# The last store of a fused attention and gated-MLP kernel, in two partition halves from two engines

## The chip, the cores and the metric

The kernel runs on one core of a Trainium2 chip. A core has TensorE (matrix products, into PSUM), VectorE, ScalarE and GpSimd (elementwise work), SyncE, which here issues the transfers, and 16 DMA engines that move data between HBM and the on-chip SBUF. Engines run their own instruction lists and wait for each other by semaphores. The metric is the device time of one execution in microseconds (us); the kernel before takes 222.05 us (median of 3 runs, 221.95 to 222.31).

## The reference

The input x is 2048 tokens by 512 columns. It is normalised once, goes through two branches, and both results are added to x:

```
xn = layernorm(x)                                   # 2048 x 512, bf16
# A: linear attention, 32 heads of 16
q, k, v = split(xn @ wqkv)
phi(t)  = [softmax(t @ w_phi), softmax(-(t @ w_phi))]     # 32 features per head
o       = phi(q) @ (phi(k)^T v) / (phi(q) @ sum(phi(k)) + 1e-6)
A       = o @ wo
# B: gated MLP, 512 -> 1792 -> 512
B       = ((xn @ w_gate) * (xn @ w_up)) @ w_down
out     = x + A + B
```

The output has the shape of x, in bf16: 2 MB.

## The kernel before, in words

Tokens are handled in 16 tiles of 128 (`NT`), in four groups of four. After the loads, a first phase normalises the tiles, makes keys and values, and sums phi(k)^T v over all tiles; units of the gated MLP (`unit`, lines 268 to 280; one of 14 column blocks for one group of 512 tokens) are mixed in so that TensorE always has work. A second loop (lines 444 to 453) goes over the tiles again: `attend(n)` makes the attention result of a tile and has it transposed by a DMA, `qproj` prepares a later tile, and `fin(n - 2)` finishes a tile that is two behind. The order on every engine and on the DMA queue is the order of the program text (line 102 takes the planning out of the framework's hands), so what is written last runs last on each engine.

`fin(n, cuts)` (lines 287 to 300) does the last step for one tile. For each stretch of output columns between two cuts it accumulates 14 products of the MLP with `w_down` (line 293) and 4 of the attention with `wo` (line 296) in one PSUM bank, adds x on VectorE into the bf16 tile `o_sb` (line 299), and stores it (line 300). For 15 tiles there is one stretch of 512 columns. The last tile is called with cuts at 0, 384 and 512 (line 456), so that its last store has 128 columns: 128 partitions (token rows) by 256 bytes, 32 KB.

All transfers in this kernel, loads, transposes and stores, are issued by SyncE (`nc.sync`); ScalarE issues none. SyncE's stores are preceded in its list by the transposes of the attention tiles. After the last store SyncE's list has only the waits at the end of the program (line 482), in which it waits for all transfers before the engines meet in a barrier.

Of the kernel before, what the change touches and what calls it, by code (L numbers as in the profile page):

```python
# [21 lines left out]
def kernel(  # L22
# [12 lines left out]
    nc = tc.nc  # L35
    P = 128
    S, D = A_x.shape[-2], A_x.shape[-1]
# [12 lines left out]
    def token_views(ap):  # L50
        rows = ap.flatten_outer_dims()
        first = rows[0:TT, :].rearrange("(n p) d -> p n d", p=P)
        rest = rows[TT:S, :].rearrange("(p n) d -> p n d", p=P)
        return lambda lo, hi: first[:, lo:hi, :] if hi <= GT else rest[:, lo - GT:hi - GT, :]

    x_view = token_views(A_x)
    out_view = token_views(out)
# [29 lines left out]
    for lo in (0, 2):  # L87
        nc.sync.dma_start(out=wv[:, lo:lo + 2, :],
                          in_=A_wqkv[lo * P:(lo + 2) * P, 2 * D:3 * D].rearrange("(c p) f -> p c f", p=P))
# [58 lines left out]
    def bank(name, dt=F32, n=TT):  # L148
        return ps_s.tile([P, n], dt, name=name, tag="s")
# [137 lines left out]
    def fin(n, cuts=(0, D)):  # L287
        T, t4 = n // GT, n % GT
        for lo, hi in zip(cuts, cuts[1:]):
            w = hi - lo  # L290
            ps = bank("fin")[:, 0:w]
            for f in range(FC):
                nc.tensor.matmul(ps, lhsT=hTs[T][:, f, t4 * P:(t4 + 1) * P], rhs=wd[:, f, lo:lo + w],  # L293
                                 start=(f == 0), stop=False)
            for c in range(DC):
                nc.tensor.matmul(ps, lhsT=oTs[n][:, c, :], rhs=wo[:, c, lo:lo + w],  # L296
                                 start=False, stop=(c == DC - 1))
            o_sb = opool.tile([P, w], BF16, name=f"o_sb{w}")
            nc.vector.tensor_tensor(out=o_sb[:], in0=ps, in1=xall[:, n, lo:lo + w], op=ALU.add)  # L299
            nc.sync.dma_start(out=out_view(n, n + 1)[:, 0, lo:lo + w], in_=o_sb[:])  # L300


    warm = bank("warm")
# [120 lines left out]
    with tc.tile_pool(name="ps_ab", bufs=1, space=PSUM) as ps_ab, \  # L424
# [19 lines left out]
        for n in range(NT):  # L444
            attend(n)
            if n + 5 < NT:
                qproj(n + 5)
            if n < 2:
                ffn(2 - n)
                continue  # L450
            fin(n - 2)
            if n >= 4:
                ffn(2)
        ffn(len(units))
        fin(NT - 2)
        fin(NT - 1, cuts=(0, 3 * P, D))


# [28 lines left out]
```

## Time and profile before

The profile is of one execution, taken by the hardware profiler.

| what | value |
|---|---|
| median of 3 runs | 222.05 us (221.95 to 222.31) |
| the profiled execution's own time | 221.94 us |
| its span, first to last instruction | 220.2 us |
| TensorE busy | 214.5 us, 97% of the span |
| VectorE, ScalarE, GpSimd busy | 63%, 40%, 33% |
| granted clock of TensorE (mean) | 0.998 |
| stores | 15 of 128 KB, one of 96 KB, one of 32 KB |
| last addition on VectorE | 217.50 to 217.79 us |
| last store issued | 217.82 us |

How to read it: a row of the timeline has the start in us from the span's start, the duration, the engine (PE is TensorE, DVE is VectorE, ACT is ScalarE, SPq is SyncE's issuing of DMAs), the source line, the operation with output and inputs, and behind the bracket what ended the engine's idle time. An issue row is the time in which the engine hands the transfer over, not the time in which the data move. "To landing" is from the start of the issue to the last report of the DMA engines that the data are there; each of the 16 engines reports by raising the store's semaphore by one. In a table of stretches the columns are the stretch, its length and TensorE's busy time (with the number of instructions), then weight loads, VectorE, ScalarE and GpSimd, the granted clock, the share of the 16 DMA engines and GB/s.

### The profile page before, as it was taken

Reading aid. Unit: us, or ns where it says so; the run is one execution under the profiler, and the core shown is the slowest. Engines: PE = TensorE matmul, PEld = TensorE weight load, DVE = VectorE, ACT = ScalarE, POOL = GpSimd, SP = SyncE. Lnnn points to the kernel's source line nnn. Section 1 sums busy time; section 2 is a strip of 40 time slices with the busy share of each in tenths; the row PEclk is TensorE's granted clock in tenths of the full one; section 3 lists DMA queues with packets and bytes.
Section 4 is the critical chain, followed back from the end, with each engine's and each line's share of the span. In section 5 each row is a group of like instructions: output and inputs, shape, how many; then the busy total and the mean of one; then the engine's idle time right before and its main releaser. Section 6 shows DMA issues by size and latency. Waiting matters only on the chain.

```text
span 220.2 us, 3489 instructions
## 1 busy us (share of the span) xinstructions
PE 214.5 (97%) x1285; PEld 104.4 (47%) x1309; DVE 138.4 (63%) x237; ACT 88.2 (40%) x162; POOL 72.1 (33%) x62
## 2 busy tenths in 40 slices
PE   7999999999999999999999999999999999999995
PEld 2564444445444444444544444444444444454443
DVE  5657985885579685756589964197655745445321
ACT  2635486559755876545354221231322323100000
POOL 5300555455336653536333633033033033000000
PEclk9999999999999999999999999999999999999999
DMA  5999994404201223010205945214431431522611
GB/s 171 261 306 383 368 225 59 95 1 49 49 0 33 42 54 65 18 34 0 48 1 100 119 95 113 58 24 95 98 72 24 95 71 27 91 53 71 69 30 48
DMA packets 47233, 19.91 MB, mean 90 GB/s; under 512 B 37488, under 2 KB 46960, under 8 KB 47088
## 3 DMA queue, kind: packets, MB, share of 16 engines
q1 hardware_dynamic: 47216, 19.69, 39.6%
q8 instruction: 10, 0.16, 0.3%
q14 instruction: 7, 0.06, 0.1%
HBM read 8.67 MB, written 2.10 MB: 49 GB/s over the span
## 4 chain that ended last, share of the span: by engine, by line
PE 94%; DVE 2%; DMA 1%; issue 1%; POOL 0%; ACT 0%; DVEq 0%
PE fin L293 22%; PE u L275 22%; PE g L275 21%; PE fin L296 6%; PE pv L240 6%; PE q L240 6%; PE k L240 6%; PE ab L430 2%; PE kv L333 2%; DMA xall<-in_A_x_dram 1%; DVE stats L155 1%; PE pq L231 1%; DVE sums L252 1%; PE tp L213 0%; DVE hT L280 0%
## 5 line engine op out<-in xcount | busy, mean ns | idle before, releaser
L275 PE MATMUL u<-xnT,wu 128*128 128x512 bf16 (+1 forms) x229 | 57.7, 372 | 0.4
L275 PE MATMUL g<-xnT,wg 128*128 128x512 bf16 (+1 forms) x222 | 56.7, 371 | 0.4
L280 DVE TENSOR_TENSOR hT<-u,g_sb 128x512 bf16<-128x512 f32 (+1 forms) x58 | 37.4, 649 | 27.3 <-PE u L275 18.0
L279 ACT CAST g_sb<-g 128x512 bf16<-128x512 f32 (+1 forms) x58 | 33.3, 573 | 48.2 <-PE g L275 48.1
L252 DVE TENSOR_REDUCE sums<-e 128x64 f32<-128x1024 f32 x32 | 38.9, 1215 | 20.7 <-ACT e L249 20.7
L293 PE MATMUL fin<-wd,hT 128*128 128x512 bf16 (+2 forms) x234 | 50.9, 366 | 0.3
L256 POOL TENSOR_TENSOR phiq<-e,rs 128x1024 bf16<-128x1024 f32 x16 | 31.0, 1935 | 61.4 <-DVE rs L254 53.1
L256 POOL TENSOR_TENSOR phik<-e,rs 128x1024 bf16<-128x1024 f32 x16 | 30.9, 1934 | 48.2 <-DVE rs L254 46.2
L275 PEld LDWEIGHTS <-wu 128*128 128x128 bf16 x232 | 22.6, 98 | 25.7
L293 PEld LDWEIGHTS <-hT 128*128 128x128 bf16 x238 | 22.4, 98 | 24.8
L275 PEld LDWEIGHTS <-wg 128*128 128x128 bf16 x232 | 21.9, 98 | 23.4
L240 PEld LDWEIGHTS <-xnT 128*128 128x128 bf16 x192 | 17.3, 97 | 18.2 <-ACT xnT L215 1.1
L299 DVE TENSOR_TENSOR o_sb<-fin,xall 128x512 bf16<-128x512 f32 (+2 forms) x17 | 11.2, 656 | 22.3 <-PE fin L296 22.2
L248 ACT ACTIVATE e<-q 128x512 f32<-128x512 f32 x16 | 9.5, 596 | 26.1 <-PE q L240 20.7
L254 DVE RECIPROCAL rs<-sums 128x64 f32<-128x64 f32 x32 | 17.7, 553 | 3.1
L240 PE MATMUL pv<-wv,xnT 128*128 128x512 bf16 x62 | 16.4, 379 | 0.4 <-ACT xnT L215 0.2
L296 PE MATMUL fin<-wo,oT 128*128 128x512 bf16 (+2 forms) x68 | 16.6, 366 | 0.0
L240 PE MATMUL k<-W1k,xnT 128*128 128x512 bf16 x63 | 16.2, 379 | 0.0
L240 PE MATMUL q<-W1q,xnT 128*128 128x512 bf16 x60 | 15.9, 378 | 0.1
L322 ACT CAST vt<-pv 128x512 bf16<-128x512 f32 x14 | 8.3, 591 | 10.9 <-PE pv L240 10.9
L248 ACT ACTIVATE e<-k 128x512 f32<-128x512 f32 x16 | 9.6, 597 | 7.0 <-PE k L240 6.6
L439 DVE TENSOR_TENSOR otok<-ab,rden 128x512 bf16<-128x512 f32 x16 | 11.1, 691 | 0.6
(46 smaller groups left out, 117.4 us busy)
## 6 DMA issues: line engine op xcount, KB each, us to landing
out_dram<-o_sb SPq DMA_DIRECT2D x15, 128.0 KB, 1.9
wd<-in_B_w_down_dram SPq DMA_DIRECT2D x1, 1792.0 KB, 15.4
wg<-in_B_w_gate_dram SPq DMA_DIRECT2D x2, 640.0 KB, 7.0
wu<-in_B_w_up_dram SPq DMA_DIRECT2D x2, 640.0 KB, 8.1
xall<-in_A_x_dram SPq DMA_DIRECT2D x1, 1024.0 KB, 12.0
wv<-in_A_wqkv_dram SPq DMA_DIRECT2D x2, 256.0 KB, 3.9
wg<-in_B_w_gate_dram SPq DMA_DIRECT2D x2, 256.0 KB, 4.9
wu<-in_B_w_up_dram SPq DMA_DIRECT2D x2, 256.0 KB, 5.3
```

Of the source, the lines that this page charges most:

```text
L240: nc.tensor.matmul(ps, lhsT=xnT[:, j, n * P:(n + 1) * P], rhs=w[:, j, :], start=(j == 0), stop=(j == DC - 1))
L248: nc.scalar.activation(out=e[:, :, 0, :], in_=pfv, func=AF.Exp, scale=1.0)
L252: nc.vector.tensor_reduce(out=sums[:], in_=ev, axis=AX.X, op=ALU.add)
L254: nc.vector.reciprocal(out=rs[:].rearrange("p a b -> p (a b)"), in_=sums[:])
L256: nc.gpsimd.tensor_tensor(out=phi[:].rearrange("p g (x f) -> p (g x) f", f=DH), in0=ev, in1=rs[:].to_broadcast((P, 2 * H, DH)), op=ALU.mult)
L275: nc.tensor.matmul(ps, lhsT=w[:, c, f * P:(f + 1) * P], rhs=xnT[:, c, T * TT + lo:T * TT + hi], start=(c == 0), stop=(c == DC - 1))
L279: nc.scalar.copy(out=g_sb[:, 0:hi - lo], in_=pss[0])
L280: nc.vector.tensor_tensor(out=hTs[T][:, f, lo:hi], in0=pss[1], in1=g_sb[:, 0:hi - lo], op=ALU.mult)
L293: nc.tensor.matmul(ps, lhsT=hTs[T][:, f, t4 * P:(t4 + 1) * P], rhs=wd[:, f, lo:lo + w], start=(f == 0), stop=False)
L296: nc.tensor.matmul(ps, lhsT=oTs[n][:, c, :], rhs=wo[:, c, lo:lo + w], start=False, stop=(c == DC - 1))
L299: nc.vector.tensor_tensor(out=o_sb[:], in0=ps, in1=xall[:, n, lo:lo + w], op=ALU.add)
L439: nc.vector.tensor_tensor(out=o_tok[:].rearrange("p (b h d) -> p b h d", b=2, d=DH), in0=abv[:, :, :, 0:DH], in1=rden[:].to_broadcast((P, ...
```

## The change

In `fin`, the store of a stretch stays as it is, except for the last stretch of a tile that is cut more than once. That is one store in the whole program: columns 384 to 511 of tile 15. It is issued as two: partitions 0 to 63 of `o_sb` by SyncE, partitions 64 to 127 by ScalarE. Each has 64 rows of 256 bytes, 16 KB, and goes to its own rows of the output.

```diff
@@ -297,7 +297,11 @@
                                  start=False, stop=(c == DC - 1))
             o_sb = opool.tile([P, w], BF16, name=f"o_sb{w}")
             nc.vector.tensor_tensor(out=o_sb[:], in0=ps, in1=xall[:, n, lo:lo + w], op=ALU.add)
-            nc.sync.dma_start(out=out_view(n, n + 1)[:, 0, lo:lo + w], in_=o_sb[:])
+            if hi < D or len(cuts) == 2:
+                nc.sync.dma_start(out=out_view(n, n + 1)[:, 0, lo:hi], in_=o_sb[:])
+            else:
+                for eng, rows in ((nc.sync, slice(0, P // 2)), (nc.scalar, slice(P // 2, P))):
+                    eng.dma_start(out=out_view(n, n + 1)[rows, 0, lo:hi], in_=o_sb[rows, :])
```

## The prediction

> **What bounds the kernel now.** I read the page's first and fourth parts first (busy shares, and the chain that ended last), then the timeline of the last microseconds, then the queue's issues and what the queue waited for, and last a table of stretches over the two stores that can be told apart. The page says which engine carries the run:
>
> ```profile
> span 220.2 us, 3489 instructions
> PE 214.5 (97%) x1285; PEld 104.4 (47%) x1309; DVE 138.4 (63%) x237; ACT 88.2 (40%) x162; POOL 72.1 (33%) x62
> ...
> PE 94%; DVE 2%; DMA 1%; issue 1%; POOL 0%; ACT 0%; DVEq 0%
> ...
> out_dram<-o_sb SPq DMA_DIRECT2D x1, 96.0 KB, 1.6
> out_dram<-o_sb SPq DMA_DIRECT2D x1, 32.0 KB, 1.4
> ```
>
> TensorE is busy for 97% of the span and makes 94% of the chain; nothing in this change touches it. What is left for a change of the last store is the stretch after the last matmul. The two store rows differ from the other fifteen: 96 KB and 32 KB, because the last tile is cut at column 384; the 32 KB one is the store in question, and it lands 1.4 us after its issue. The timeline of the end:
>
> ```profile
> 216.50 0.56 DVE L299 TENSOR_TENSOR o_sb<-fin,xall 128x384 bf16<-128x384 f32 x1 [2.23 <-PE fin L296]
> ...
> 217.08 0.39 PE L296 MATMUL fin<-wo,oT 128*128 128x128 bf16 x4
> ...
> 217.50 0.29 DVE L299 TENSOR_TENSOR o_sb<-fin,xall 128x128 bf16<-128x128 f32 x1 [0.45 <-PE fin L296]
> ...
> 217.82 0.33 SPq L300 DMA_DIRECT2D out_dram<-o_sb  x1
> ```
>
> The last matmuls end at about 217.47, the last addition runs from 217.50 to 217.79, and SyncE issues the last store from 217.82 to 218.15. After that only this store is under way. What ends it is in the queue's own waits over the last 4 us:
>
> ```profile
> SPq L300 <- DVE o_sb L299: 2.7, 2, 2.4
> SPq L482 <- DMA out_dram<-o_sb: 1.0, 1, 1.0
> SPq L482 <- PEq L482: 0.6, 2, 0.4
> ```
>
> L482 is the end of the program, where SyncE waits for every transfer; 1.0 us of that is the wait for this store. ScalarE is free for the new issue: its last instruction in the whole trace is this one, 29 us before the end:
>
> ```profile
> 188.12 0.59 ACT L279 CAST g_sb<-g 128x512 bf16<-128x512 f32 x1 [1.14 <-PE g L275]
> ```
>
> Stretches of the store of 128 KB issued at 210.41 (first four rows) and of the last store (the others); the last two columns are the share of the 16 DMA engines and GB/s:
>
> ```profile
> 210.41:210.74 0.33, 0.33 (x3) 0.14 (x2) 0.00 (x0) 0.00 (x0) 0.00 (x0) 1.00 0.00 0
> 210.74:211.23 0.49, 0.49 (x4) 0.21 (x3) 0.00 (x0) 0.00 (x0) 0.00 (x0) 1.00 0.00 0
> 211.23:211.76 0.53, 0.53 (x4) 0.28 (x3) 0.00 (x0) 0.00 (x0) 0.00 (x0) 1.00 0.73 247
> 211.76:212.11 0.35, 0.35 (x4) 0.13 (x2) 0.00 (x0) 0.00 (x0) 0.00 (x0) 1.00 0.00 0
> 217.82:218.15 0.33, 0.00 (x0) 0.00 (x0) 0.00 (x0) 0.00 (x0) 0.00 (x0) 1.00 0.63 205
> 218.35:218.64 0.29, 0.00 (x0) 0.00 (x0) 0.00 (x0) 0.00 (x0) 0.00 (x0) 1.00 0.00 0
> 218.64:218.92 0.28, 0.00 (x0) 0.00 (x0) 0.00 (x0) 0.00 (x0) 0.00 (x0) 1.00 0.55 117
> 218.92:219.26 0.34, 0.00 (x0) 0.00 (x0) 0.00 (x0) 0.00 (x0) 0.00 (x0) 1.00 0.00 0
> 219.26:220.19 0.93, 0.00 (x0) 0.00 (x0) 0.00 (x0) 0.00 (x0) 0.00 (x0) 0.60 0.00 0
> ```
>
> So a store is made of four parts. For the last one: issue 0.33 (the traffic seen in that row is the 96 KB store before it, whose packets end at 218.34), then 0.49 in which nothing moves, 0.28 of packets, 0.34 until the last of its 16 engines has reported: 1.44 us, 217.82 to 219.26. The store of 128 KB has the same 0.33 and 0.49, 0.53 of packets, and its last report 1.69 after its start. Only the packet part scales with size. Behind the last report come 0.93 us of closing waits and barriers.
>
> **The change part by part.** One store of 128 rows by 256 bytes becomes two of 64 rows by 256 bytes. The bytes, the matmuls, the addition and all earlier stores stay: the test in the code holds only for the last piece of the last tile.
>
> Size alone. From 32 to 128 KB the time to the last report grows from 1.44 to 1.69, 0.25 us for 96 KB, that is 0.0026 us per KB. A 16 KB half would by that line land in 1.44 - 0.04 = 1.40 us. Carried to no bytes at all, the line leaves 1.35, so the whole possible gain from less data per store is below 0.09 us, and 0.04 is my value, since half of the 32 KB remains in each.
>
> Both halves meet on the same engines. In the packet records the store's 128 rows are 8 packets of 256 bytes on each of 16 engines, 18 ns each at a pitch of about 14 ns. If the halves run together over all 16, each engine has the same eight to move, and even the 0.04 is not there; I keep it as the lower end.
>
> A rule of the Trainium skill speaks against this edit: "DMA: Bandwidth & Descriptors", section "Rules for kernel authors", says of two transfers to disjoint partition halves not to bother, as both spread over the same 16 engines, and to use one transfer of 128 partitions. The trace shows the 16 reports per store, but no pair of halves; by the rule the size term is 0 in place of -0.04.
>
> SyncE's issue. Its row is 0.33 us whether the store has 128, 96 or 32 KB, all with 128 rows. I cost the half at the same 0.33. A shorter issue could come with half the rows: the first loads took 0.40 with 128 rows, 0.43 to 0.47 with 256, and up to 0.51 with 512, about 0.03 per 128 rows, so at most 0.02 us; left out. Nothing is queued behind it on SyncE but the closing waits.
>
> ScalarE's issue, the unknown. No row of this trace has a DMA issued by ScalarE, and all 47,216 data packets ran in one queue. Work on ScalarE hides nothing here and blocks nothing: it has been waiting at the closing barrier since about 188.7, and both issues are released by the same event, the end of the addition at 217.79. Behind ScalarE's issue stands only its part of the barrier, which is not needed before about 219.5. The question is only how much later the second half's last report comes.
> Lower end: the two issues run side by side and the second half is no later, 0.
> Upper end: the two go as two issues in a row do on one queue. The first two loads of x have 128 rows each, were issued at 0.789 and 1.249, and had their last reports at 2.879 and 3.394: 0.515 us apart.
> The pair of loads is the nearest row, as two transfers asked for at once. But of its 0.515, 0.06 is the gap between the two issues on one sequencer, 0.07 is the difference between an issue of 0.40 that had not waited and one of 0.33 that had, and the rest contains larger packets. What remains is one issue, 0.33 us, and I take that: the second half starts to be prepared when the first has been.
>
> A second rule bears on this. "Perfetto Trace Analysis", section "DMA Instruction — HWDGE (DVE, Sync)", says that the descriptor generator is shared by the issuing sequencers and locked for exclusive use by one of them. No run here shows it yet; by it the second half waits for the first's generation, at most the 0.33 issue row, and without it the term would be 0.
>
> The closing waits. SyncE takes five waits of two semaphores each in a fixed order; the last store's semaphore is in the third, and each further wait costs about 0.065 us (219.317, 219.379, 219.444 are the starts that follow). The stores' semaphores go round in order (109, 110, 101 for the last three), so the new one would be 102, which stands in the second wait. If 102 reports last, three waits instead of two follow it: +0.06; if it is taken into a later wait, 0. I take 0.06. All the rest of the 0.93 is unchanged.
>
> Sum against the profiled execution, 221.94 us (its span 220.19 and 1.75 around it): -0.04 + 0.33 + 0.06 = +0.35, 222.29 us. That execution is 0.11 under the median of 222.05, so on the median I forecast 222.40 us, +0.16%. A measurement of this kernel tells about 0.2%, 0.44 us, from no change: the three runs spread over 0.36 us.
>
> **The rivals.**
> Side by side. The two halves are prepared and moved together, and the second is not late: -0.04 + 0.06 = +0.02, 222.07 us. For it: 16 DMA engines stand idle from 218.34, and ScalarE has been idle for 29 us. Against it: the pair of loads, which were 0.515 apart with 16 engines just as free.
>
> Slower, by the first use of ScalarE's queue. This is the first and only transfer on that queue, released at the one place where nothing covers it. For it: SyncE's own first load had its first packet 1.03 us after its issue began (1.820 from 0.789), the isolated stores 0.83; that is 0.20 more. Against it: that row is a load, and its following ones were slow as well. Price: the forecast's 0.35 + 0.20 = +0.55, 222.60 us. It decides from 0.09 us on top of the forecast's sum, where the 0.44 is passed. Work around the span for one more queue would belong to the same case; the 1.75 us there now are not divided by any row.
>
> The split gains. The second half would have to be on time, the size term would have to reach its end of 0.09, and no wait would be added: -0.09, 221.96 us. Against it stands that issue, pause and report, 1.16 of the 1.44 us, do not depend on the size in the two stores compared. It cannot pass -0.44 by itself.
>
> That the change does nothing is no case: the condition is met for exactly one piece, and both halves are stored.
>
> **How the numbers follow.** One after the other, 0.42; side by side, 0.32; first use, 0.20; gain, 0.06. Run-to-run scatter is up to 0.26 us above the median. With it about a third of the first case passes 0.44 (0.14), almost all of the third (0.17), and little of the second (0.03): slower 0.34. Faster comes from the fourth and from scatter in the second: 0.06. Same: 0.60. For the range, the low end is the gain case at 221.96 less a little scatter, 221.90. The high end takes the upper bounds: 0.515 - 0.04 + 0.06 + 0.20 = 0.735, 222.79, and most of the scatter, 223.00.
>
> **What the profile of the changed kernel would show.** Right: three store rows of 96, 16 and 16 KB; the ScalarE issue about as long as SyncE's plus a wait, or starting its packets some 0.3 us after the first half's; the last report near 219.55 in place of 219.26, and the addition still ending at 217.8. Side by side would show both halves' packets in the same 0.28 us. First use would show a pause of more than 0.5 us between ScalarE's issue and its first packet, or a span unchanged and a longer time around it. The prediction is wrong if ScalarE's issue takes much longer than 0.33 us, or if anything before 217 moves.

## The result, and the profile after

The changed kernel takes 222.94 us (median of 6 runs, 222.82 to 223.25) against 222.03 us before (median of 6 runs, 221.95 to 222.64). The ratio is 1.0032, with a 95% interval of 1.0022 to 1.0042: slower by 0.5 to 0.9 us. In a second comparison on one chip the same kernel gave 1.0037 (1.0025 to 1.0050). The time lies in the forecast range, but on its upper edge, and the case that I held likeliest was too small.

The queues and the last instructions in the profile of the changed kernel (line 301 is now the ordinary store, line 304 the two halves, line 486 the end of the program). First, two rows of the page; the queue row's columns are packets, MB and the share of the 16 engines:

```profile
span 221.1 us, 3515 instructions
...
q10 hardware_dynamic: 80, 0.02, 0.0%
```

ScalarE's half has a queue of its own, 64 packets of data and 16 reports. Then the timeline of the end, SyncE's, VectorE's and ScalarE's rows:

```profile
217.77 0.29 DVE L299 TENSOR_TENSOR o_sb<-fin,xall 128x128 bf16<-128x128 f32 x1 [0.45 <-PE fin L296]
...
218.09 0.56 SPq L304 DMA_DIRECT2D out_dram<-o_sb  x1
...
218.10 0.57 ACTq L304 DMA_DIRECT2D out_dram<-o_sb  x1
```

Both issues begin within 4 ns of each other, 0.03 us after the addition has ended, as intended. But each takes 0.56 us where the single store took 0.33. What SyncE's queue waited for at the end, and the issues with their sizes and time to landing:

```profile
SPq L486 <- DMA out_dram<-o_sb: 1.4, 2, 1.1
```

```profile
out_dram<-o_sb SPq DMA_DIRECT2D x1, 96.0 KB, 1.6
out_dram<-o_sb SPq DMA_DIRECT2D x1, 16.0 KB, 1.8
out_dram<-o_sb ACTq DMA_DIRECT2D x1, 16.0 KB, 2.0
```

The closing wait for the last store has grown from 1.0 to 1.4 us in two waits. The 96 KB store is as before; 16 KB now take 1.8 and 2.0 us where 32 KB took 1.4. In stretches (the last columns are the share of the 16 DMA engines and GB/s, as before the change):

```profile
218.06:218.66 0.60, 0.00 (x0) 0.00 (x0) 0.00 (x1) 0.00 (x0) 0.00 (x0) 1.00 0.52 164
218.66:219.30 0.64, 0.00 (x0) 0.00 (x0) 0.00 (x0) 0.00 (x0) 0.00 (x0) 1.00 0.00 0
219.30:219.57 0.27, 0.00 (x0) 0.00 (x0) 0.00 (x0) 0.00 (x0) 0.00 (x0) 1.00 0.34 62
219.57:219.79 0.22, 0.00 (x0) 0.00 (x0) 0.00 (x0) 0.00 (x0) 0.00 (x0) 1.00 0.41 74
219.79:220.14 0.35, 0.00 (x0) 0.00 (x0) 0.00 (x0) 0.00 (x0) 0.00 (x0) 1.00 0.00 0
220.14:221.08 0.94, 0.00 (x0) 0.00 (x0) 0.00 (x0) 0.00 (x0) 0.00 (x0) 0.74 0.00 0
```

The traffic in the first row is again the 96 KB store. Then nothing moves for 0.64 us; SyncE's packets start at 219.30 and ScalarE's at 219.57, one group after the other and not together; 0.35 us after the last packet comes the last report, and the closing part takes 0.93 us as before. So in the two profiles the stretch from the end of the last addition to the end of the span is 2.40 us before and 3.01 after, +0.61. I call it the tail.

The spans differ by 0.89 us, since the last addition itself ends 0.27 us later (218.06 against 217.79). That part is not of the change: it is there at 11 us (VectorE begins its first copy of values into `vt`, line 322 before and 326 now, at 10.72 and at 10.99), long before the first store at 128 us, and stays to the end. What makes it is open. It arises while the first loads land, whose reports differ from profile to profile (the second load of `wv` at 6.95 and 7.23 us here), but that one load does not decide it: in the profile of e3 below it reports at 6.53, and the last addition ends at 218.46. Over the 14 profiles of this study the last addition ends anywhere from 217.79 to 218.50 us, and the kernel before is at the early end. So single profiles are compared below by their tails, and times by the ratios, which have several runs on each side. The tail's 0.61 lies inside the interval of the ratio, which is 0.49 to 0.93 us; the medians are 0.91 apart.

All of the kernels whose last store was changed, in one table (us; "issue" and "last report" count from that store's own start; S is SyncE, A is ScalarE):

| kernel | issue | last report | addition to last report | tail | ratio (95%) |
|---|---|---|---|---|---|
| before, 128 rows by S | S 0.33 | 1.44 | 1.47 | 2.40 | |
| the change, 64 by S, 64 by A | S 0.56, A 0.57 | 1.78, 2.05 | 2.08 | 3.01 | 1.0032 (1.0022 to 1.0042) |
| the change again (e12) | S 0.56, A 0.58 | 1.78, 2.04 | 2.07 | 3.00 | 1.0037 (1.0025 to 1.0050) |
| both halves by S (e1) | S 0.55, S 0.58 | 1.78, 1.80 | 2.43 | 3.43 | 1.0050 (1.0035 to 1.0065) |
| whole, by A (e2) | A 0.37 | 1.49 | 1.52 | 2.47 | 0.9998 (0.9988 to 1.0007) |
| the change, A's queue used before (e3) | S 0.56, A 0.56 | 1.77, 2.03 | 2.06 | 3.00 | 1.0030 (1.0018 to 1.0042) |
| S's 64 rows alone (e4) | S 0.56 | 1.78 | 1.80 | 2.76 | |
| column halves by S and A (e6) | S 0.33, A 0.37 | 1.42, 1.58 | 1.61 | 2.56 | 1.0014 (1.0004 to 1.0023) |
| 96 by S, 32 by A (e8) | S 0.35, A 0.39 | 1.48, 1.64 | 1.67 | 2.63 | 1.0009 (1.0000 to 1.0019) |
| A's 64 rows alone (e9) | A 0.55 | 1.77 | 1.80 | 2.76 | |
| 64 by S, 32 by A (e10) | S 0.56, A 0.38 | 1.78, 1.42 | 1.81 | 2.83 | |
| 80 by S, 48 by A (e11) | S 0.35, A 0.39 | 1.45, 1.61 | 1.64 | 2.59 | 1.0005 (0.9996 to 1.0014) |

### The profile page after: what moved, and what is told of

Same layout as the page of the kernel before. It is cut to its first block, busy times and chain, and to the rows that moved or that the text cites. A ratio compares the mean times of both kernels' runs of the same rounds, so it can differ in the third digit from the quotient of the medians.

```text
span 221.1 us, 3515 instructions
## 1 busy us (share of the span) xinstructions
PE 216.2 (98%) x1309; PEld 104.7 (47%) x1309; DVE 138.4 (63%) x237; ACT 88.2 (40%) x162; POOL 72.0 (33%) x62
## 4 chain that ended last, share of the span: by engine, by line
PE 95%; DMA 2%; SPq 1%; issue 0%; DVE 0%
PE g L275 22%; PE u L275 22%; PE fin L293 22%; PE fin L296 6%; PE q L240 6%; PE k L240 6%; PE pv L240 6%; DMA wv<-in_A_wqkv_dram 2%; PE ab L434 2%; PE kv L337 2%; PE pq L231 1%; SPq L75 1%; SPq L88 0%; PE tp L213 0%; DVE o_sb L299 0%
## 5 line engine op out<-in xcount | busy, mean ns | idle before, releaser
L275 PE MATMUL g<-xnT,wg 128*128 128x512 bf16 (+1 forms) x232 | 57.9, 372 | 0.0
```

Source lines behind the costliest of these rows:

```text
L275: nc.tensor.matmul(ps, lhsT=w[:, c, f * P:(f + 1) * P], rhs=xnT[:, c, T * TT + lo:T * TT + hi], start=(c == 0), stop=(c == DC - 1))
```

## The experiments

My first theory was that two issues open at once slow each other, 0.33 becoming 0.56. The rivals were the first use of ScalarE's queue, and that a store of 64 rows is slow by itself. The edits are shown against the kernel before or, where a removed line has the condition or the two halves, against the change; where the condition is not shown, it is that of the change, so that only the last store is concerned.

**e1, both halves by SyncE**

```diff
-                for eng, rows in ((nc.sync, slice(0, P // 2)), (nc.scalar, slice(P // 2, P))):
+                for eng, rows in ((nc.sync, slice(0, P // 2)), (nc.sync, slice(P // 2, P))):
```

> Both halves are issued by SyncE, one after the other; ScalarE issues nothing. Theory 1 (two issues that are open at once slow each other, 0.33 us becomes 0.56): here they cannot be open at once, so each issue row is 0.33 to 0.41 us, the first half's last report comes 1.40 to 1.44 us after its issue as in the single store, the second's issue begins about 0.38 us later and its last report comes about 1.8 to 1.95 us after the first issue began (2.05 in the change, 1.44 in the kernel before). Theory 2 (ScalarE's queue is late because it is used once): the same rows as theory 1. Theory 3 (a store of 64 rows is slow in itself): the first half has an issue of 0.56 us and its last report at about 1.78. Time: 222.4 to 222.6 by 1 and 2, over 222.8 by 3.

Measured: the issue rows are 0.553 and 0.577 us and the last reports 1.776 and 1.801 us after their own starts; the second issue begins 0.605 us after the first, and the tail is 3.43 us. The timeline shows both issues in one row, and the issues' list their landing:

```profile
218.49 1.18 SPq L304 DMA_DIRECT2D out_dram<-o_sb  x2
```

```profile
out_dram<-o_sb SPq DMA_DIRECT2D x2, 16.0 KB, 1.8
```

The first issue was open alone and still took 0.55. Theory 1 falls here, and the numbers are those of theory 3. It also shows what ScalarE is good for: its half in the change ended 0.35 us earlier than a second half behind SyncE's first (2.08 against 2.43).

**e2, the whole store by ScalarE**

```diff
-                nc.sync.dma_start(out=out_view(n, n + 1)[:, 0, lo:hi], in_=o_sb[:])
+                nc.scalar.dma_start(out=out_view(n, n + 1)[:, 0, lo:hi], in_=o_sb[:])
```

> The last store is whole, 128 rows, and issued by ScalarE alone. Theory 1 (two issues open at once slow each other): issue 0.33 us, first packet 0.83 us and last report 1.44 us after the issue began, as from SyncE; the time is that of the kernel before within 0.1 us, but for 0 to 0.1 us in the closing waits. Theory 2 (first use of ScalarE's queue): the first packet comes 1.0 us or more after the issue began and the last report 1.6 to 2.05, time 222.2 to 222.7. Theory 3 (64 rows are slow): as theory 1.

Measured: issue 0.369 us, first packet 0.871 after the issue began (0.823 from SyncE), last report 1.485 (1.437); the ratio is 0.9998 (0.9988 to 1.0007).

```profile
218.07 0.37 ACTq L303 DMA_DIRECT2D out_dram<-o_sb  x1
```

The one and only transfer of that queue costs 0.05 us more than SyncE's. First use is not the cause.

**e3, the change with ScalarE's queue used 3.5 us before**

```diff
-            if hi < D or len(cuts) == 2:
-                nc.sync.dma_start(out=out_view(n, n + 1)[:, 0, lo:hi], in_=o_sb[:])
+            if hi < D or len(cuts) == 2:
+                eng = nc.scalar if n == NT - 2 else nc.sync
+                eng.dma_start(out=out_view(n, n + 1)[:, 0, lo:hi], in_=o_sb[:])
```

> The change, and the store of tile 14, 4 us earlier, is issued by ScalarE too, so that the queue is in use before the last store. Theory 1 (two issues open at once slow each other): the two last issues again take 0.56 us each and their last reports come at about 1.78 and 2.05 us; time as the change, 222.8 to 223.0. Theory 2 (first use): ScalarE's second store has its first packet 0.83 us after its issue and both last reports lie within 1.5 us; time 222.1 to 222.3. Tile 14's own store shows first use by itself: 1.69 us to its last report from SyncE, 1.9 or more by theory 2.

Measured: the last two stores have issues of 0.558 and 0.557 and last reports at 1.774 and 2.030, as in the change; the ratio is 1.0030 (1.0018 to 1.0042). Tile 14's whole store by ScalarE took 1.750 to its last report, and 1.70 to 1.71 from SyncE in the other profiles. Together with e2 this closes the first-use rival.

**e4, SyncE's half alone**

```diff
-                nc.sync.dma_start(out=out_view(n, n + 1)[:, 0, lo:hi], in_=o_sb[:])
+                nc.sync.dma_start(out=out_view(n, n + 1)[0:P // 2, 0, lo:hi], in_=o_sb[0:P // 2, :])
```

> SyncE's half alone: rows 64 to 127 of the last 128 columns of tile 15 are left out and not stored, and ScalarE issues nothing. Theory 1 and theory 2: issue 0.33 us or a little less, first packet at 0.83, last report at 1.39 to 1.44. Theory 3 (64 rows are slow in themselves): issue 0.56, last report at 1.78.

Measured: issue 0.562, first packet 1.202, last report 1.777.

```profile
218.23 0.56 SPq L303 DMA_DIRECT2D out_dram<-o_sb  x1
```

```profile
out_dram<-o_sb SPq DMA_DIRECT2D x1, 16.0 KB, 1.8
```

No second store, no ScalarE, half of the data, and the store ends 0.34 us later than the whole one. Theory 3 holds. The next question was what is slow about 64 rows.

**e5, stores of other shapes**

```diff
-            nc.sync.dma_start(out=out_view(n, n + 1)[:, 0, lo:lo + w], in_=o_sb[:])
+            forms = {9: (P // 2, 0), 10: (96, 0), 11: (32, 0), 12: (16, 0), 13: (112, 0), 14: (P // 2, 2)}
+            rows, parts = forms.get(n, (P, 0))
+            dst, src = out_view(n, n + 1)[0:rows, 0, lo:hi], o_sb[0:rows, :]
+            if parts:
+                dst = dst.rearrange("p (a c) -> p a c", a=parts)[:, :, 0:P]
+                src = src.rearrange("p (a c) -> p a c", a=parts)[:, :, 0:P]
+            nc.sync.dma_start(out=dst, in_=src)
```

> Six of the single stores of 512 columns, each alone on SyncE, are cut to other shapes, and the rest of their rows is left out and not stored: tile 9 has 64 rows, tile 10 has 96, tile 11 has 32, tile 12 has 16, tile 13 has 112, and tile 14 has 64 rows in two separate runs of 128 columns each (128 runs in all). The last tile's two stores are those of the kernel before, 128 rows. Measured so far: 128 rows, issue 0.33 us, last report 1.44 to 1.70; 64 rows of 256 bytes, 0.56 and 1.78. Theory 3a (any store of fewer than 128 rows takes the slow way): 0.56 us in all six, also in the 64 rows with two runs. Theory 3b (it is the number of runs per DMA engine, 4 in place of 8): tile 14's form has 8 per engine and goes back to 0.33; tile 13's with 7 is between. Theory 3c (the cost grows with the missing rows, 0.23 us for 64): 0.36 to 0.39 with 112 rows, 0.45 with 96, 0.68 with 32, 0.73 with 16.

Measured: the issue rows of tiles 9 to 14, that is 64, 96, 32, 16, 112 rows, and 64 rows in two runs (two separate stretches of each row):

```profile
193.85 0.57 SPq L306 DMA_DIRECT2D out_dram<-o_sb  x1
...
197.99 0.37 SPq L306 DMA_DIRECT2D out_dram<-o_sb  x1
...
202.12 0.32 SPq L306 DMA_DIRECT2D out_dram<-o_sb  x1
...
206.27 0.32 SPq L306 DMA_DIRECT2D out_dram<-o_sb  x1
...
210.41 0.32 SPq L306 DMA_DIRECT2D out_dram<-o_sb  x1
...
214.29 0.68 SPq L306 DMA_DIRECT2D out_dram<-o_sb  x1
```

All three of my theories missed. The price does not grow with the missing rows (16 rows cost 0.32), it is not met by every store under 128 rows, and 128 runs do not help when they stand in 64 rows (0.68). The first packets agree: 1.20 us after the start for 64 rows, 1.32 for 64 rows in two runs, and 0.81 to 0.85 for 96, 32, 16 and 112.

**e7, more shapes**

```diff
-            nc.sync.dma_start(out=out_view(n, n + 1)[:, 0, lo:lo + w], in_=o_sb[:])
+            forms = {9: (0, 48), 10: (0, 80), 11: (32, 96), 12: (0, 120), 13: (0, 60), 14: (0, 8)}
+            a, b = forms.get(n, (0, P))
+            nc.sync.dma_start(out=out_view(n, n + 1)[a:b, 0, lo:hi], in_=o_sb[a:b, :])
```

> As the other study of shapes: single stores of 512 columns, each alone on SyncE, in other shapes, with the rest of their rows left out and not stored. Tile 9 has rows 0 to 47, tile 10 rows 0 to 79, tile 11 rows 32 to 95 (64 rows that begin elsewhere), tile 12 has 120 rows, tile 13 has 60, tile 14 has 8. So far 16, 32, 96, 112 and 128 rows took 0.32 to 0.37 us to issue and 64 rows 0.55 to 0.57. Theory 4a (exactly 64 rows take a slow way, wherever they begin): only tile 11 has 0.56 us and a first packet at 1.2; the five others have 0.31 to 0.40 and 0.82 to 0.90. Theory 4b (the 64 rows are slow because they fill one half of the partitions, 0 to 63 or 64 to 127): tile 11 is fast too. Theory 4c (a middle range of row counts is slow): tiles 9, 10 and 13 are slow as well.

Measured, tiles 9 to 14 with 48, 80, 64 (rows 32 to 95), 120, 60 and 8 rows:

```profile
194.30 0.34 SPq L302 DMA_DIRECT2D out_dram<-o_sb  x1
...
198.44 0.32 SPq L302 DMA_DIRECT2D out_dram<-o_sb  x1
...
202.58 0.63 SPq L302 DMA_DIRECT2D out_dram<-o_sb  x1
...
206.72 0.40 SPq L302 DMA_DIRECT2D out_dram<-o_sb  x1
...
210.86 0.33 SPq L302 DMA_DIRECT2D out_dram<-o_sb  x1
...
214.74 0.28 SPq L302 DMA_DIRECT2D out_dram<-o_sb  x1
```

Only tile 11 is slow, with its first packet at 1.27 us; the others start at 0.75 to 0.84. Of the ten row counts tried (8, 16, 32, 48, 60, 64, 80, 96, 112, 120) 64 alone is slow, and it is slow at rows 0 to 63, 32 to 95 and 64 to 127, with 256 and 1024 bytes a row, from both engines (0 to 63 and 32 to 95 from SyncE only). In the whole study all 14 issues of 64 rows, in nine profiles, took 0.55 us or more. Theory 4a holds as a description, for the counts tried: most of the others stand on one or two rows, and none between 60 and 80 but 64 was tried. Why 64 differs is not shown by any run, and I leave it open. It was tried for stores to HBM only.

**e6, halves by columns**

```diff
+                for eng, a in ((nc.sync, 0), (nc.scalar, w // 2)):
+                    eng.dma_start(out=out_view(n, n + 1)[:, 0, lo + a:lo + a + w // 2], in_=o_sb[:, a:a + w // 2])
```

> The last store is halved by columns in place of rows: all 128 rows by 64 columns (128 bytes) from SyncE, the other 64 columns from ScalarE, issued at once as in the change. It tells what two issues at once cost when neither has 64 rows. If the price of the change is the 64-row form (0.34 us) and the order of the two (0.27 us) as separate terms: SyncE's issue is back at 0.33 and its last report at 1.40 to 1.45 us, ScalarE's last report follows 0.2 to 0.35 us later, at about 1.7, and the time is 0.25 to 0.35 us over the kernel before, a ratio of 1.001 to 1.002. If two issues at once slow each other in any form: both issues are over 0.5 us and the last report is at 1.9 or later, a ratio of 1.0025 or more. If the two run side by side: 1.45 for both, ratio 1.000.

Measured: issues 0.332 and 0.370 us, first packets 0.828 and 0.902 after their starts, last reports 1.420 and 1.578; ratio 1.0014 (1.0004 to 1.0023).

```profile
218.52 0.33 SPq L304 DMA_DIRECT2D out_dram<-o_sb  x1
```

```profile
218.53 0.37 ACTq L304 DMA_DIRECT2D out_dram<-o_sb  x1
```

Two issues of 128 rows, open at the same time, are as long as each alone (0.33 and 0.37): neither lengthened the other's row. ScalarE's data end 0.08 us after SyncE's and its last report 0.16 after. The order of the two halves thus costs less here than the 0.2 to 0.35 that I had carried over from the change, though the ratio lies in the range that was given for it.

**e8 and e11, parts of 96 and 32 and of 80 and 48 rows**

```diff
-                for eng, rows in ((nc.sync, slice(0, P // 2)), (nc.scalar, slice(P // 2, P))):
+                for eng, rows in ((nc.sync, slice(0, 96)), (nc.scalar, slice(96, P))):
```

> The change with its two parts of 96 rows (SyncE) and 32 rows (ScalarE) in place of 64 and 64; all is stored. If the 64-row form is what the change pays for: issues of 0.33 to 0.37 us, SyncE's last report at 1.42 to 1.45 us, ScalarE's at 1.40 to 1.60, the stretch from the last addition to the end of the span 2.40 to 2.55 us (2.40 before, 3.01 in the change), time within 0.15 us of the kernel before, ratio 0.999 to 1.0007. If two row parts from two engines are slow whatever their size: issues over 0.5 us, the stretch 2.9 us or more, ratio over 1.002.

> The change with parts of 80 and 48 rows, the nearest to halves among the row counts that were fast alone. If exactly 64 rows are the price: both issues 0.32 to 0.40 us, SyncE's last report at 1.45 to 1.50 us, ScalarE's at 1.58 to 1.66, the stretch from the last addition to the end 2.55 to 2.65 us (2.63 with 96 and 32 rows, 3.01 in the change), ratio 1.0005 to 1.0015. If it is a matter of nearly equal parts: issues over 0.5, the stretch 2.9 or more, ratio near that of the change beside it.

Measured for 96 and 32: issues 0.347 and 0.391, last reports 1.483 and 1.642, tail 2.63 (I had 2.40 to 2.55), ratio 1.0009 (1.0000 to 1.0019). For 80 and 48, with 80 and 48 in the same place of the edit: 0.347 and 0.391, 1.447 and 1.606, tail 2.59, ratio 1.0005 (0.9996 to 1.0014). For 96 and 32 the last reports, the tail and the ratio are all above what I had given; for 80 and 48, forecast after it, they came as expected.

```profile
out_dram<-o_sb SPq DMA_DIRECT2D x1, 20.0 KB, 1.4
out_dram<-o_sb ACTq DMA_DIRECT2D x1, 12.0 KB, 1.6
```

The same split between the same two engines, 16 rows off the middle, loses 0.42 of the change's 0.61 us of tail. What is left, 0.19, comes with the second store from a second engine: it is also there with columns (0.17) and with 96 and 32 (0.23). No run has two stores of these shapes from one engine, so the share of the engine is not told apart from that of the second store. In e8 the last packets end 1.12 and 1.15 us after the starts; ScalarE's last report then takes another 0.49 us, 0.44 in e6 and 0.47 in e11, where a store alone needs about 0.35. So in these three runs, where the packets of two stores move at the same time, the wait for the later one's report is longer; why is not shown.

**e9, ScalarE's half alone**

```diff
-                nc.sync.dma_start(out=out_view(n, n + 1)[:, 0, lo:hi], in_=o_sb[:])
+                nc.scalar.dma_start(out=out_view(n, n + 1)[P // 2:P, 0, lo:hi], in_=o_sb[P // 2:P, :])
```

> ScalarE's half alone: rows 64 to 127 of the last 128 columns of tile 15; rows 0 to 63 of them are left out and not stored, and SyncE does not issue in their place. In the change ScalarE's half had its first packet 1.47 us and its last report 2.05 us after its issue began. If 0.27 us of that are waiting for SyncE's half: 1.21 to 1.27 for the first packet and 1.78 to 1.83 for the last report. If ScalarE's own 64-row store is that slow: 1.47 and 2.05 again.

Measured: issue 0.548, first packet 1.195, last report 1.771; in the change 0.567, 1.473 and 2.047.

```profile
218.49 0.55 ACTq L303 DMA_DIRECT2D out_dram<-o_sb  x1
```

```profile
out_dram<-o_sb ACTq DMA_DIRECT2D x1, 16.0 KB, 1.8
```

So ScalarE's half is 0.28 us later in the change than alone, and this comes from SyncE's half beside it.

**e10, 64 rows by SyncE and 32 by ScalarE**

```diff
-                for eng, rows in ((nc.sync, slice(0, P // 2)), (nc.scalar, slice(P // 2, P))):
+                for eng, rows in ((nc.sync, slice(0, 64)), (nc.scalar, slice(64, 96))):
```

> SyncE issues rows 0 to 63 and ScalarE at the same moment rows 64 to 95; rows 96 to 127 of the last 128 columns of tile 15 are left out and not stored. A store of 32 rows alone has its first packet 0.82 us after its issue. If what both engines share is held while SyncE's 64 rows are prepared: ScalarE's first packet comes after SyncE's, over 1.2 us. If each engine prepares its own and the slowness of 64 rows is its own: ScalarE's first packet at 0.82 to 0.95, its last report at 1.5 or before, and SyncE's stays at 1.78.

Measured: ScalarE's 32 rows have their first packet 0.883 us after the issue and their last report at 1.421; SyncE's 64 rows 1.197 and 1.782.

```profile
out_dram<-o_sb SPq DMA_DIRECT2D x1, 16.0 KB, 1.8
out_dram<-o_sb ACTq DMA_DIRECT2D x1, 8.0 KB, 1.4
```

Started together, the 32 rows have their first packet 0.31 us ahead of the 64 rows and their last report 0.36 us ahead. While a 64-row store is prepared, another engine's store of a common shape is not held up; a second 64-row store is (e9 against the change). What the two of them share is not shown.

**e12, the change again**

The edit is the change itself.

> The change itself, beside the split in 80 and 48 rows and the kernel before on one chip. By its earlier profile: issues of 0.56 us, last reports at 1.78 and 2.05, the stretch from the last addition to the end 3.01 us against 2.40 before, ratio 1.0025 to 1.0035; the end of the last addition may lie anywhere from 217.8 to 218.5, as in the other profiles, since it follows the loads at the start.

Measured: 0.558 and 0.575, 1.775 and 2.035, tail 3.00, ratio 1.0037 (1.0025 to 1.0050). On the same chip the split of 80 and 48 gave 1.0005; the two intervals do not meet.

No version here beats the kernel before. The nearest is the whole store from ScalarE (e2), which cannot be told from it. By its time nor can the split of 80 and 48 rows, but its tail is 0.19 us longer.

## Why the prediction was right and wrong

The time, 222.94 us, is inside 221.90 to 223.00. But the median forecast was 222.40, within 0.2% of the kernel before, and the measured change is beyond it; the 0.34 for slower was the case that came. That the range holds is partly luck: with the scatter that I allowed, 0.26 us, the forecast reaches 222.66, below every run of the change (222.82 to 223.25). The range went up to 223.00 by a wider gap between the halves and by first use of a queue, and neither is what cost the time.

By the signs that it named, the prediction was wrong in its mechanism: ScalarE's issue was to stay near 0.33 us and took 0.57. Another sign, ScalarE's packets some 0.3 us after the first half's, came true (0.27). The sign for first use, a pause of more than 0.5 us between ScalarE's issue and its first packet, came too (0.91), and it would have misled: it is the same 0.91 in e3, where the queue had been used, and SyncE's half has 0.64. What moved before 217 us, the 0.27 of the last addition, had done so since the loads.

Step by step, against the tail:

- **What bounds the end** was right: the last store alone decides the end (the 96 KB store before it, still moving at 217.8, has its last report at 218.70), nothing on TensorE changed, and ScalarE was free. Its issue began 4 ns after SyncE's.
- **"Size alone"** (-0.04) and **"SyncE's issue"** (half the rows at the same 0.33) are the steps that failed. I drew a line through two stores of 128 rows and carried it to 64 rows, a shape with no row in the trace. Measured for SyncE's half: issue 0.56, last report 1.78, +0.35 in place of -0.04 (e4 alone gives +0.34). Half the rows was a new form of the instruction, and I bounded its price above by that of the whole one. The miss of this term, 0.39 us, is more than the 0.26 by which the sum missed the tail. Nor was the 0.33 a fixed price of 128 rows in the trace that I had: it holds for the stores from tile 9 on (0.33 to 0.37), while the first nine, each handed over 0.1 us after a transpose, took 0.49 to 0.53 (the rows are in the last section).
- **"ScalarE's issue, the unknown"** (+0.33) was near in size: the second half's last report came 0.27 us after the first's. That is partly luck, since it was not right as a general price. In e6, e8 and e11, two stores of other shapes end 0.16 us apart, and their issues overlap in full; the pair of loads that I took it from shows one sequencer working through two issues.
- **The closing waits** (+0.06): none in the change. The 0.93 us stayed, because the semaphore in the later wait (101) went to ScalarE's store and 102 to SyncE's. In e1, where 102 came last, the closing part is 1.00 us, so the price was right and its place was not.
- **Sum:** +0.35 was forecast, from -0.04, +0.33 and +0.06; the tail has +0.35, +0.27 and 0, that is +0.61.
- **Rival "first use"** ended near the right time, 222.60, for a wrong reason: a store from ScalarE costs 0.05 us more (e2), and using its queue earlier helps nothing (e3).
- **Rival "side by side"** is what happens with other row counts, though not quite: +0.19 in place of +0.02 for 80 and 48 rows.
- **The two rules of the Trainium skill.** The advice of "DMA: Bandwidth & Descriptors", "Rules for kernel authors", not to halve by partitions, was right in direction. Its reason is that the two halves serialize, since both use the same 16 engines. The packets of the two 64-row halves did move one after the other (ScalarE's start 0.04 us after SyncE's have ended), but those of the column halves moved together (SyncE's from 0.83 to 1.06 us, ScalarE's from 0.90 to 1.14). Sharing engines could cover at most the 0.17 to 0.23 us that the other splits cost here, not the 0.35 of a 64-row store that is alone (e4); the row says nothing of 64 rows. "Perfetto Trace Analysis", section "DMA Instruction — HWDGE (DVE, Sync)", has the generator locked by one issuing engine at a time. Here two issues open at once were 0.33 and 0.37 us, as long as alone (e6), and a 32-row store passed a 64-row one (e10). As a lock over the whole issue row it does not agree with these runs. Where the two stores have 64 rows, the 0.27 would fit something that one of them holds, but not inside the issue row: ScalarE's, 0.57, is hardly longer than alone (0.55, e9).

## What to carry to other kernels

A store at the very end costs mostly its fixed parts: 1.16 of 1.44 us were the same with four times the data, so cutting it brings almost nothing, and in three splits without 64 rows a second store from a second engine added about 0.2 us. A duration from the trace holds for the instruction's shape too: when an edit changes the number of rows, that is a new operation, and its price is open on both sides. Where the time of a store to HBM counts, as here at the end, stores of exactly 64 partitions are worth avoiding: 48, 80 or 128 took the short way.

## What the runs showed of the hardware that was not expected

Of eleven row counts from 8 to 128, 64 alone is slow: 0.55 to 0.63 us for the issue (0.68 in two runs per row) against 0.28 to 0.42, and for a store alone the first packet 1.20 to 1.27 us after the issue began (1.32 in two runs) against 0.75 to 0.92. Why is open.

These are stores from tile 9 on, handed over more than a microsecond after the last transpose. The row count is not the only thing that lengthens an issue. In the kernel before, each of the first nine stores, all with 128 rows, was handed over 0.1 us after a transpose and took 0.49 to 0.53 us, with its first packet at 1.04 to 1.09. The last of the nine, and the next one:

```profile
186.80 1.23 SPq L263 DMA_TRANSPOSE phiqT<-phiq  x1
188.12 0.53 SPq L300 DMA_DIRECT2D out_dram<-o_sb  x1
...
193.85 0.34 SPq L300 DMA_DIRECT2D out_dram<-o_sb  x1
```

The slow 64-row stores had no transpose so close before them.

ScalarE, which had issued nothing before, hands over a store 0.04 us more slowly than SyncE (0.37 against 0.33). Stores of 112 and 120 rows are handed over quickly, but their last reports came at 1.85 and 1.95 us. In the place of the 112 rows, 128 rows took 1.69 to 1.71 in the other profiles; in the place of the 120 rows they took 1.71 to 1.89. I did not follow that up.
